# Two fused feed-forward blocks behind a retention layer: another order of block products, activations split on VectorE, first form weights loaded earlier

## The chip, the core and the metric

The kernel runs on one core of one Trainium2 chip. The metric is the time of one execution on the device in microseconds (us). Engines are named as in the profile: PE is TensorE (PEld its weight loads), DVE is VectorE, ACT is ScalarE, POOL is GpSimd, SP is SyncE, which here only issues DMAs.

## What is computed

```python
# retention: state = gamma * state + k v^T ; y = scale * q state   (4 batches, 8 heads, 768 steps, 64 wide)
x = attn_out.transpose(0, 2, 1, 3).reshape(B * S, H * D)        # 3072 x 512
h = x @ moe_w_in            # 512 -> 2048
g = np.maximum(0.01 * h, h)
x = g @ moe_w_out           # 2048 -> 512
h = x @ moe2_w_in           # 512 -> 2048
g = h - np.tanh(h)
return g @ moe2_w_out       # 2048 -> 512
```

Everything is float32. A product of float32 matrices is made of three matmuls on split operands: high part by high part, high by low and low by high, where the high part is the value rounded to the matmul's format and the low part is the rest.

## The kernel before

After the retention layer come four matrix products. The two that widen (512 to 2048) are done by a Strassen-Winograd scheme: a group is a pair of 128-row blocks of the hidden dimension, and instead of eight block products it takes seven, P1 to P7 (table PROD: form of the weight, form of the activation, PSUM bank). One block product is 6 matmuls of 128x128 by 128x512. The two that narrow (2048 to 512) are outer products: step o takes one 128-row block of activations and adds to four PSUM banks, in two halves of 6 matmuls each. The first narrowing product is o = 0 to 95, the second o = 96 to 191.

The stretch that the change is about starts when 48 outer products of the first narrowing product are done (ND_FROM). From there on PE alternates: 168 block products of the second widening product (24 groups d of seven, built by `prod`) and 288 halves of outer products (`half_unit`), about 1.7 halves behind each product, until the products are used up; 56 halves and one more are left for the end. A product or a half is called a unit here: 456 units, the last 57 without products.

What stands around a unit:

- Weights. The seven forms of a group were made earlier by DVE and ACT (`form_sets`) and stored to DRAM (`wfs`, `put_forms`, 7 DMAs on SP). `load_f(i)` loads the weights `wf` of product i, four products ahead (F_AHEAD).
- Activations of outer product o. `load_g` loads `gr`, three outer products ahead; `split_g(o + 2)` makes the high part `gh` on ACT (L151) and the low part `gl` = gr - gh on an engine that it is told (L152): DVE up to o = 49, POOL after that.
- Results of a group. The bank X of group d (two banks in turn) holds P1, then on top of it P6, P7 and P4; Y (one bank) holds P5, then P3; Z holds P2. ACT copies the sum after P1, P5 and P6 to SBUF (`kp`, L889), and DVE adds: P2 with the copy of P1, P3 with that of P6, P7 with that of P5 (`h`, L896). P4 ends in the bank and is read there. A product that adds to a bank waits for the copy or addition that still reads it.
- Elementwise. From each of the four sums of a group h - tanh(h) is made (`queue_el`): four ACT instructions (`eu`, `et`, `es`, `mk`), on DVE `ew` twice (L924, L927), `es` (L930) and a predicated copy (L942), for three of four a DMA on POOL that adds h to `et` (L958). The result is stored (`g2s`) and comes back as `gr` of the second narrowing product.
- Weights of the second narrowing product: `second_out` makes `w2h` (ACT, L823) and `w2l` (DVE, L825) from `w2r`.

Everything is written in program order by a planner. After each unit `background` adds a credit of 1.29 us x 1.05 to each of "a" (ACT) and "v" (DVE), capped at 2.0; copies and additions of due products are written at once and charged; then the other queues are written as long as their credit is over zero, in this order for DVE: forms of the next activations (`bx`), elementwise, then weight forms, `second_out` and conversions. ACT's and DVE's work runs in the order so written, each engine in turn. SBUF tiles come from a list of free slots, first in, first out (`alloc`, `give`); a tile waits for the last reader of its slot.

The order of the seven products of a group is written in line 798; P4' stands for P4 of the group before.

Of the kernel before, what the change touches and what calls it, by code (L numbers as in the profile page):

```python
# [9 lines left out]
F32 = mybir.dt.float32  # L10
F32R = mybir.dt.float32r
# [44 lines left out]
PROD = {  # L56
    "P1": ("A11", "B11", "X", 0),
    "P2": ("A12", "B21", "Z", 1),
    "P5": ("S1", "T1", "Y", 2),
    "P6": ("S2", "T2", "X", 4),  # L60
    "P3": ("S4", "B22", "Y", 5),
    "P7": ("S3", "T3", "X", 10),
    "P4": ("N22", "T4", "X", 13),
}
FORMS = ("A11", "A12", "S1", "S2", "S3", "S4", "N22")
NG = NM // 2
NSB = NC // 2
SPAN = 7 * NG

ND_FROM, N_TAIL, UNIT_US = 3 * NM, 28, 1.29  # L70
C_AHEAD, M_AHEAD, F_AHEAD, F_LOW = 5, 3, 4, 5
# [3 lines left out]
def kernel(  # L75
# [12 lines left out]
    nc = tc.nc  # L88
# [17 lines left out]
    wfs = dr.tile([NG, 7, P, 2, 2 * P], F32, tag="wfs", name="wfs")  # L106
# [5 lines left out]
    def alloc(nm, dt=F32, shape=(P, TB)):  # L112
        pool, tag = free.popleft()
        serial[0] += 1
        t = pool.tile(list(shape), dt, tag=tag, name=f"{nm}_{serial[0]}")
        home[id(t)] = (t, pool, tag)
        return t

    def give(*ts):
        for t in ts:  # L120
            _, pool, tag = home.pop(id(t))
            free.append((pool, tag))
# [5 lines left out]
    def run(queues, us):  # L128

        while us > 0:  # L130
            for queue in queues:
                cost = next(queue[0], "end") if queue else None
                if cost is not None:
                    break
            if cost is None:
                return 0.0
            if cost == "end":
                queue.popleft()
            else:
                us -= cost  # L140
        return us
# [7 lines left out]
    def split(hi, lo, src, eng):  # L149

        nc.scalar.activation(out=hi, in_=src, func=AF.Copy)  # L151
        eng.tensor_tensor(out=lo, in0=src, in1=hi.bitcast(F32), op=ALU.subtract)  # L152
# [57 lines left out]
    def conversion(units, ready=None, ahead=RAW_BUFS - 1):  # L210

        while ready and not ready():
            yield None
        last = len(units)
        at = {}
        raws[0] += 1

        def load(n):
            if n < last:
                units[n].load()  # L220
                at[n] = tick[0] + LOAD_LEAD

        for n in range(ahead):
            load(n)
        for n in range(last + 2):
            if n >= 2:
                yield from units[n - 2].done(units[n - 2])
            if n < last:
                while tick[0] < at[n] or len(free) < 3:
                    yield None  # L230
                units[n].s1()
            if 1 <= n <= last:
                yield from units[n - 1].s2()
                load(n - 1 + ahead)
        raws[0] -= 1
# [33 lines left out]
    formed = set()  # L269
# [356 lines left out]
    def where_g(o):  # L626

        if o < NT:
            return o // NM, o % NM
        nb, i = divmod(o - NT, NM)  # L630
        return nb, i // 2 + i % 2 * NG

    def load_g(o):
        if o < 2 * NT:
            nb, m = where_g(o)
            assert o < NT or (nb, m) in made2, (nb, m)
            GR[o] = alloc("gr")
            nc.sync.dma_start(out=GR[o], in_=(g1s if o < NT else g2s)[nb, m])

    def split_g(o, eng):  # L640
        if o < 2 * NT:
            G[o] = alloc("gh", F32R), alloc("gl", F32R)
            split(*G[o], GR[o], eng)
            give(GR.pop(o))

    def mm_half(o, half):
        nb, m = where_g(o)
        first, last = o % NM == 0, o % NM == NM - 1
        js = (2 * half, 2 * half + 1)
        base = 0 if o // NM in (1, 2 * NC - 1) else 4  # L650
        g = G[o]
        for j in js:
            if first:
                ACC[j] = bank(base + j, f"o_{o // NM}_{j}")
            c = slice(j * P, (j + 1) * P)
            if o < NT:
                w = WO[m]
                three = ((w[0][:, c], g[0]), (w[0][:, c], g[1]), (w[1][:, c], g[0]))
            else:
                w = WE[m]  # L660
                three = ((g[0][:, c], w[0]), (g[0][:, c], w[1]), (g[1][:, c], w[0]))
            for i, (a, b) in enumerate(three):
                nc.tensor.matmul(ACC[j], a, il(b), start=first and i == 0, stop=last and i == 2)  # L663
        if half:
            give(*G.pop(o))
            if nb == NC - 1 and o < NT:
                give(*WO.pop(m))
# [20 lines left out]
    def step(o):  # L688
        for half in range(2):
            mm_half(o, half)  # L690
            evac(o, half)
# [74 lines left out]
    for i, (at_, sb, g, nm) in enumerate(stream):  # L766
# [13 lines left out]
        if xleft:  # L780
            c, p = xleft.pop(0)
            t = xw.pop((c, p))
# [12 lines left out]


    dnow = [-1]
    order = [(d, nm) for d in range(NSB * NG) for nm in ("P1", "P4'", "P2", "P5", "P6", "P3", "P7")]
    order = [(d - 1, "P4") if nm == "P4'" else (d, nm) for d, nm in order if nm != "P4'" or d]
    order.append((NSB * NG - 1, "P4"))  # L800
    place = {x: i for i, x in enumerate(order)}
    NPROD = len(order)
# [3 lines left out]
    def second_out():  # L806
        rl, arrive = {}, {}

        def fetch(i):
            if i < NM:  # L810
                rl[i] = alloc("w2r")
                nc.sync.dma_start(out=rl[i], in_=w2s[use_in[i]])
                arrive[i] = tick[0] + LOAD_LEAD

        fetch(0)
        fetch(1)
        for i, m in enumerate(use_in):
            fetch(i + 2)
            while tick[0] < arrive[i] or len(free) < 10:
                yield None  # L820
            hi, lo = alloc("w2h", F32R), alloc("w2l", F32R)
            src = rl[i].rearrange("p (b a) -> p a b", a=2)
            nc.scalar.activation(out=hi.rearrange("p (a b) -> p a b", a=2), in_=src, func=AF.Copy)  # L823
            yield 0.0
            nc.vector.tensor_tensor(out=lo.rearrange("p (a b) -> p a b", a=2), in0=src,  # L825
                                    in1=hi.rearrange("p (a b) -> p a b", a=2).bitcast(F32), op=ALU.subtract)
            give(rl.pop(i))
            WE[m] = hi, lo
            yield 0.7

    conv.append(conversion(conv2_in + conv2[W2_EARLY:]))
    at_n = [0]
# [21 lines left out]
    for n in range(ND_FROM):  # L854
        load_g(n + C_AHEAD if n + C_AHEAD < ND_FROM + M_AHEAD else 2 * NT)
        if n == 0:
            split_g(2, nc.vector)
            continue
        while n % NM not in WO:
            tick[0] += 1  # L860
            run((conv,), 0.01)
        step(n)
        at_n[0] = n
        split_g(n + 2, nc.vector)
        tick[0] += 2
        us = run((loads, bx, forms, conv), min(us + 1.85, 1.9))


    FW, KP, XB = {}, {}, {}

    def load_f(i):
        if i < NPROD:
            d, nm = order[i]
            assert d % NG in formed, d
            t = alloc("wf", F32R)
            nc.sync.dma_start(out=t.bitcast(F32).rearrange("p (n c) -> p n c", n=2), in_=wfs[d % NG, FORMS.index(PROD[nm][0])])  # L876
            FW[i] = t

    events = {}

# [112 lines left out]
    credit = {"a": 0.0, "v": 0.0}  # L993
# [26 lines left out]
    def background():  # L1020
        for f in events.pop(tick[0], ()):
            a, v = f()
            credit["a"] -= a
            credit["v"] -= v
        credit["a"] = min(credit["a"] + UNIT_US * 1.05, 2.0)
        credit["v"] = min(credit["v"] + UNIT_US * 1.05, 2.0)
        run((loads,), 0.01)
        spend((bx,))
        while (masks[0] < 2 and drain(mk_q, "a")) or drain(act_q, "a"):
            pass  # L1030
        while drain(cp_q, "v") or drain(dve_q, "v"):
            pass
        spend((forms, bo, conv) if tick_o[0] >= NT - 14 else (forms, conv))

    tick_o = [ND_FROM]
    for i in range(F_AHEAD):
        load_f(i)
    split_done = [ND_FROM + 2]
    halves = deque((o, half) for o in range(ND_FROM, 2 * NT) for half in range(2))
    n_mid = len(halves) - 2 * N_TAIL  # L1040
    i = gone = since = 0

    def half_unit():
        o, half = halves.popleft()
        tick_o[0] = o
        if half == 0:
            load_g(o + M_AHEAD)
        while o >= NT and where_g(o)[1] not in WE:
            tick[0] += 1
            background()  # L1050
        mm_half(o, half)
        tick[0] += 1
        evac(o, half)
        if half == 0:
            split_g(o + 2, nc.gpsimd)
        background()

    while i < NPROD or halves:
        if i < NPROD:
            d, nm = order[i]  # L1060
# [9 lines left out]
        while halves and (i == NPROD or gone < i * n_mid / NPROD):  # L1070
            o, half = halves[0]
# [59 lines left out]
```

## Time and profile before

| what | us |
|---|---|
| median of 3 runs | 1110.67 |
| lowest and highest run | 1108.86, 1111.59 |
| the profiled execution, its own time | 1111.41 |
| its span, first to last instruction | 1109.6 |
| PE busy | 1061.0 (96%) |
| DVE busy | 826.4 (74%) |
| ACT busy | 691.5 (62%) |
| POOL busy | 294.1 (27%) |

The profiled execution lasts 1.8 us longer than its span. The shares are means over a retention stretch (to about 120 us), the first widening and narrowing products, the mixed stretch from 475 us to 1032 us and an end of outer products alone; they say little of any of these.

### The profile page before, as it was taken

The numbers are of one execution on the slowest core, as the hardware profiler recorded it, in microseconds if no ns is written. First come the engines' busy times: TensorE is split into PE (matmuls) and PEld (weight loads), VectorE is DVE, ScalarE is ACT, GpSimd is POOL, SyncE is SP. The second block draws the span as 40 slices with busy tenths as digits, with TensorE's granted clock in tenths as the row PEclk, the third lists the DMA queues.
The fourth block names the chain that finished last, engine by engine and source line by source line (L and its number), as shares of the span: only waits on it lengthen the run. The fifth ranks groups of instructions, "written<-read, shape, count | busy, mean of one in ns | idle before, by whom it ended". The sixth has DMA issues, their size and how long they took to land. (4 is left out here: it accounts for less than half of the span.)

```text
span 1109.6 us, 17689 instructions
## 1 busy us (share of the span) xinstructions
PE 1061.0 (96%) x5931; PEld 911.5 (82%) x5931; DVE 826.4 (74%) x1221; ACT 691.5 (62%) x1227; POOL 294.1 (27%) x266
## 2 busy tenths in 40 slices
PE   9999899999999999889799998889999899999998
PEld 6888778888888888777688886778888788888887
DVE  3578897766888797969888789888779977677400
ACT  5766667756775555546666666776667666667540
POOL 3222000000000000023434343334334443445651
PEclk9999999999999999989899999999999999999999
DMA  9997464674769699498999986888987878888540
GB/s 223 241 268 189 165 234 176 222 266 162 257 231 306 223 377 357 167 302 280 295 299 266 300 255 190 275 253 250 280 285 194 258 228 254 228 246 262 184 162 38
DMA packets 208635, 267.68 MB, mean 241 GB/s; under 512 B 65056, under 2 KB 106144, under 8 KB 208544
## 3 DMA queue, kind: packets, MB, share of 16 engines
q1 hardware_dynamic: 197888, 247.52, 66.8%
q0 software_dynamic: 10368, 18.88, 9.8%
q8 instruction: 47, 0.77, 0.3%
q14 instruction: 44, 0.36, 0.1%
q10 hardware_dynamic: 288, 0.15, 0.1%
HBM read 161.63 MB, written 85.98 MB: 223 GB/s over the span
## 5 line engine op out<-in xcount | busy, mean ns | idle before, releaser
L152 POOL TENSOR_TENSOR gl<-gr,gh 128x512 fp32r<-128x512 f32 x142 | 201.5, 1426 | 650.2 <-ACT gh L151 619.8
L663 PE MATMUL o<-gh,wo 128*128 128x512 f32 x768 | 241.2, 381 | 2.9 <-ACT gh L151 2.9
L151 ACT ACTIVATE gh<-gr 128x512 fp32r<-128x512 f32 x192 | 118.6, 624 | 103.8 <-DMA gr<-g1s 47.0
L663 PEld LDWEIGHTS o<-gh,wo 128*128 128x128 f32 x768 | 146.1, 190 | 24.3 <-ACT gh L151 3.6
L978 PE MATMUL Xd<-xch,wf 128*128 128x512 f32 x384 | 131.8, 384 | 19.5 <-DVE h L896 8.5
L663 PE MATMUL o<-gl,wo 128*128 128x512 f32 x384 | 146.9, 382 | 1.6 <-POOL gl L152 1.2
L663 PE MATMUL o<-w2h,gl 128*128 128x512 f32 x384 | 145.7, 380 | 1.6 <-POOL gl L152 1.6
L663 PE MATMUL o<-w2h,gh 128*128 128x512 f32 x384 | 145.8, 380 | 1.4 <-ACT st L676 1.4
L663 PE MATMUL o<-w2l,gh 128*128 128x512 f32 x384 | 145.5, 379 | 0.0
L722 PE MATMUL X<-xch,wg 128*128 128x512 f32 x384 | 123.3, 381 | 3.8 <-DVE wg L166 2.6
L942 DVE COPY_PREDICATED es<-mk,et 128x512 f32<-128x512 uint16 x96 | 91.6, 962 | 41.1 <-ACT mk L920 36.8
L978 PEld LDWEIGHTS Xd<-xch,wf 128*128 128x128 f32 x384 | 73.1, 190 | 33.8 <-DVE h L896 10.9
L927 DVE SCALAR_TENSOR_TENSOR ew<-eu,ew 128x512 f32<-128x512 f32 x96 | 89.6, 933 | 3.1
L722 PEld LDWEIGHTS X<-xch,wg 128*128 128x128 f32 x384 | 72.4, 189 | 17.2 <-DVE wg L166 3.4
L908 ACT ACTIVATE eu<-h 128x512 f32<-128x512 f32 x72 | 45.0, 625 | 66.2 <-DVE h L896 65.8
L930 DVE SCALAR_TENSOR_TENSOR es<-es,ew 128x512 f32<-128x512 f32 x96 | 81.1, 844 | 5.3 <-ACT gh L151 0.5
L663 PEld LDWEIGHTS o<-gl,wo 128*128 128x128 f32 x384 | 73.0, 190 | 14.0 <-POOL gl L152 2.1
L958 POOL DMA_DIRECT2D et<-h x72 | 63.2, 886 | 77.1 <-ACT et L912 36.3
L663 PEld LDWEIGHTS o<-w2h,gl 128*128 128x128 f32 x384 | 72.6, 189 | 12.8 <-POOL gl L152 2.4
L663 PEld LDWEIGHTS o<-w2h,gh 128*128 128x128 f32 x384 | 72.6, 189 | 12.4 <-ACT st L676 1.8
L663 PEld LDWEIGHTS o<-w2l,gh 128*128 128x128 f32 x384 | 72.6, 189 | 10.2
L978 PE MATMUL Yd<-xch,wf 128*128 128x512 f32 x192 | 66.9, 389 | 9.2 <-ACT kp L889 9.0
(103 smaller groups left out, 2101.8 us busy)
## 6 DMA issues: line engine op xcount, KB each, us to landing
wf<-wfs SPq DMA_DIRECT2D x168, 256.0 KB, 4.6
g1s<-c SPq DMA_DIRECT2D x96, 256.0 KB, 2.2
gr<-g1s SPq DMA_DIRECT2D x96, 256.0 KB, 5.2
g2s<-es SPq DMA_DIRECT2D x96, 256.0 KB, 2.9
gr<-g2s SPq DMA_DIRECT2D x96, 256.0 KB, 4.5
et<-h POOLq DMA_DIRECT2D x72, 256.0 KB, 4.9
raw<-in_moe_w_in_dram SPq DMA_DIRECT2D x32, 512.0 KB, 5.7
raw<-in_moe_w_out_dram SPq DMA_DIRECT2D x32, 512.0 KB, 4.5
```

Of the source, the lines that this page charges most:

```text
L151: nc.scalar.activation(out=hi, in_=src, func=AF.Copy)
L152: eng.tensor_tensor(out=lo, in0=src, in1=hi.bitcast(F32), op=ALU.subtract)
L663: nc.tensor.matmul(ACC[j], a, il(b), start=first and i == 0, stop=last and i == 2)
L722: nc.tensor.matmul(ps, w[:, c], il(x), start=first and kt == 0 and i == 0, stop=kt == 1 and i == 2, skip_group_check=True)
L908: nc.scalar.activation(out=e["u"], in_=h, func=AF.Square)
L927: nc.vector.scalar_tensor_tensor(out=e["w"], in0=e["u"], scalar=A1, in1=e["w"], op0=ALU.add, op1=ALU.mult)
L930: nc.vector.scalar_tensor_tensor(out=e["s"], in0=e["s"], scalar=K1, in1=e["w"], op0=ALU.add, op1=ALU.mult)
L942: nc.vector.copy_predicated(out=e["s"], mask=e["mk"].bitcast(mybir.dt.uint16), data=e["th"])
L958: nc.gpsimd.dma_start(out=e["th"], in_=h, accum_op=ALU.add)
L978: nc.tensor.matmul(ps, a, il(b), start=nm in ("P1", "P2", "P5") and kt == 0 and j == 0, stop=kt == 1 and j == 2, skip_group_check=True)
```

## The change

Three edits. The order of the products of a group is P1, P5, P4', P6, P2, P3, P7 in place of P1, P4', P2, P5, P6, P3, P7. The low parts `gl` of outer products 50 to 191 are made by DVE, and the planner charges both engines for a split. The first four weight loads stand behind the last four steps of the loop before the mixed stretch, in place of behind that loop.

```diff
-    order = [(d, nm) for d in range(NSB * NG) for nm in ("P1", "P4'", "P2", "P5", "P6", "P3", "P7")]
+    order = [(d, nm) for d in range(NSB * NG) for nm in ("P1", "P5", "P4'", "P6", "P2", "P3", "P7")]
...
         step(n)
         at_n[0] = n
         split_g(n + 2, nc.vector)
+        if ND_FROM - F_AHEAD <= n:
+            load_f(n - ND_FROM + F_AHEAD)
         tick[0] += 2
...
     tick_o = [ND_FROM]
-    for i in range(F_AHEAD):
-        load_f(i)
     split_done = [ND_FROM + 2]
...
         evac(o, half)
         if half == 0:
-            split_g(o + 2, nc.gpsimd)
+            split_g(o + 2, nc.vector)
+            credit["a"] -= 0.63
+            credit["v"] -= 0.69
         background()
```

`load_f` itself is the same and only stands further up. Three places show what moves.

SP's queue where the mixed stretch begins, before the change: the weights `wf` of the first products stand behind the stores of a group's forms (`wfs`).

```order
L288 DMA wfs<-wg_5087 128x2x256
L288 DMA wfs<-wg_5088 128x2x256
L290 DMA wfs<-wg_5089 128x512
L876 DMA wf_5331<-wfs 128x512
L876 DMA wf_5333<-wfs 128x512
L876 DMA wf_5335<-wfs 128x512
L876 DMA wf_5337<-wfs 128x512
L876 DMA wf_5346<-wfs 128x512
```

The same queue now: three of the four loads stand ahead of the stores `x2s` of the last outer product's results, the fourth behind these and ahead of the forms.

```order
L638 DMA gr_5223<-g1s 128x512
L838 DMA wf_5241<-wfs 128x512
L638 DMA gr_5252<-g1s 128x512
L838 DMA wf_5270<-wfs 128x512
L838 DMA wf_5292<-wfs 128x512
L678 DMA x2s<-st_5303 128x512
L678 DMA x2s<-st_5306 128x512
L678 DMA x2s<-st_5315 128x512
L678 DMA x2s<-st_5318 128x512
L838 DMA wf_5325<-wfs 128x512
L288 DMA wfs<-wg_5083 128x2x256
```

They have moved past those stores and the seven stores of forms; the load of `gr` for outer product 50 now has one of them ahead.

DVE's work in the second group, before: elementwise instructions alone.

```order
L927 SCALAR_TENSOR_TENSOR ew_5910<-eu_5856,ew_5910 128x512
L930 SCALAR_TENSOR_TENSOR es_5869<-es_5869,ew_5910 128x512
L924 SCALAR_TENSOR_TENSOR ew_5937<-eu_5888,Xd_5582 128x512
L927 SCALAR_TENSOR_TENSOR ew_5937<-eu_5888,ew_5937 128x512
L934 TENSOR_TENSOR et_5890<-Xd_5582,et_5890 128x512
L930 SCALAR_TENSOR_TENSOR es_5892<-es_5892,ew_5937 128x512
```

And now: a `gl` about every six instructions, each of which reads the `gh` that ACT makes from the loaded `gr`.

```order
L152 TENSOR_TENSOR gl_5879<-gr_5829,gh_5878 128x512
L944 COPY_PREDICATED es_5748<-mk_1_5866,et_5739 128x512
L926 SCALAR_TENSOR_TENSOR ew_5900<-eu_5822,h_5789 128x512
L929 SCALAR_TENSOR_TENSOR ew_5900<-eu_5822,ew_5900 128x512
L944 COPY_PREDICATED es_5797<-mk_1_5892,et_5795 128x512
L932 SCALAR_TENSOR_TENSOR es_5842<-es_5842,ew_5900 128x512
L152 TENSOR_TENSOR gl_5920<-gr_5870,gh_5919 128x512
L926 SCALAR_TENSOR_TENSOR ew_5924<-eu_5894,Xd_5573 128x512
```

On DVE whatever stands behind a `gl` now waits with it for ACT and for the load of `gr`.

DVE's work where the second narrowing product begins, as it stands now: `w2l_7810` belongs to the weights of outer product 97, `gl_7820` behind it to the activations of outer product 99.

```order
L944 COPY_PREDICATED es_7687<-mk_1_7800,et_7685 128x512
L825 TENSOR_TENSOR w2l_7810<-w2r_7073,w2h_7809 128x512
L152 TENSOR_TENSOR gl_7820<-gr_7776,gh_7819 128x512
L825 TENSOR_TENSOR w2l_7829<-w2r_7075,w2h_7828 128x512
L944 COPY_PREDICATED es_7728<-mk_9_7824,et_7726 128x512
```

The weights of outer product 97 are thus written right ahead of their use, those of 98 and 99 three units and one unit ahead; before, it was 23, 22 and 24 units.

## Rows read from the trace of the kernel before

**Rows 1.** Chain that ended last, its last piece: start us, us, what.

```profile
1031.73 73.83 PE o L663 x342
```

**Rows 2.** PE's instructions in time, 455 to 490 us: start, length, what [idle before, releaser].

```profile
466.73 0.38 PE L663 MATMUL o<-gh,wo 128*128 128x512 f32 x1
475.45 0.76 PE L978 MATMUL Xd<-xch,wf 128*128 128x512 f32 x1 [8.35 <-DMA wf<-wfs]
...
480.18 0.38 PE L663 MATMUL o<-gh,wo 128*128 128x512 f32 x1
```

**Rows 3.** SP's DMA issues in time, 430 to 490 us.

```profile
465.89 2.20 SPq L678 DMA_DIRECT2D x2s<-st  x4
...
472.05 2.69 SPq L876 DMA_DIRECT2D wf<-wfs  x5
```

**Rows 4.** PE's waits from 480 to 1040 us: us in total, times, longest.

```profile
PE Yd L978 <- ACT kp L889: 9.0, 6, 2.2
PE Xd L978 <- DVE h L896: 8.5, 6, 2.7
PE o L663 <- ACT gh L151: 2.9, 1, 2.9
PE o L663 <- POOL gl L152: 2.8, 4, 0.9
PE o L663 <- ACT st L676: 1.4, 1, 1.4
PE Xd L978 <- ACT kp L889: 1.4, 2, 1.0
PE Xd L978 <- DVE et L934: 1.3, 1, 1.3
```

**Rows 5.** PE's instructions in time, 530 to 552 us.

```profile
534.79 0.38 PE L978 MATMUL Xd<-xch,wf 128*128 128x512 f32 x1
...
548.24 0.38 PE L663 MATMUL o<-gl,wo 128*128 128x512 f32 x1
```

**Rows 6.** Groups of DVE, 480 to 1040 us: shapes, xcount, busy us, mean ns, idle before.

```profile
L942 DVE COPY_PREDICATED es<-mk,et 128x512 f32<-128x512 uint16 x95 | 90.8, 964 | 41.0 <-ACT mk L920 36.6 <-DMA et<-h 4.2
L927 DVE SCALAR_TENSOR_TENSOR ew<-eu,ew 128x512 f32<-128x512 f32 x96 | 89.6, 933 | 3.1
L930 DVE SCALAR_TENSOR_TENSOR es<-es,ew 128x512 f32<-128x512 f32 x96 | 81.1, 844 | 5.3 <-ACT gh L151 0.5
L924 DVE SCALAR_TENSOR_TENSOR ew<-eu,h 128x512 f32<-128x512 f32 x72 | 64.8, 901 | 4.3 <-DMA wfs<-wg 2.8 <-ACT eu L908 1.6
...
L896 DVE TENSOR_TENSOR h<-Zd,kp 128x512 f32<-128x512 f32 x24 | 16.4, 683 | 12.4 <-PE Zd L978 9.3 <-DMA out_dram<-st 2.5 <-DMA g2s<-es 0.6
```

**Rows 7.** DVE and POOL in time, 655 to 690 us.

```profile
669.38 0.73 DVE L942 COPY_PREDICATED es<-mk,et 128x512 f32<-128x512 uint16 x1
...
669.94 1.89 POOL L152 TENSOR_TENSOR gl<-gr,gh 128x512 fp32r<-128x512 f32 x1 [0.53 <-ACT gh L151]
...
670.72 1.66 DVE L927 SCALAR_TENSOR_TENSOR ew<-eu,ew 128x512 f32<-128x512 f32 x1
...
672.41 0.69 DVE L930 SCALAR_TENSOR_TENSOR es<-es,ew 128x512 f32<-128x512 f32 x1
```

**Rows 8.** Groups of POOL, 480 to 1040 us.

```profile
L152 POOL TENSOR_TENSOR gl<-gr,gh 128x512 fp32r<-128x512 f32 x119 | 172.9, 1454 | 631.1 <-ACT gh L151 607.3 <-DMA g2s<-es 6.1 <-DMA wf<-wfs 5.4
```

**Rows 9.** Groups of DVE, 120 to 440 us.

```profile
L152 DVE TENSOR_TENSOR gl<-gr,gh 128x512 fp32r<-128x512 f32 x39 | 26.3, 684 | 15.1 <-ACT gh L151 15.1
```

**Rows 10.** Busy us (instructions) in two stretches: PE, PEld, DVE, ACT, POOL, PEclk, DMA, GB/s.

```profile
467.00:605.00 138.00, 121.78 (x532) 103.63 (x532) 115.05 (x159) 85.18 (x150) 52.24 (x41) 0.93 0.92 292
655.00:745.00 90.00, 76.99 (x343) 63.66 (x342) 77.35 (x103) 62.75 (x110) 30.75 (x27) 1.00 0.77 237
```

**Rows 11.** ACT's waits from 480 to 1040 us.

```profile
ACT gh L151 <- DMA gr<-g2s: 35.7, 20, 5.8
ACT gh L151 <- DMA gr<-g1s: 33.0, 15, 5.0
```

More of the change, by code (lines that the diff above doesn't have):

```diff
@@ L829, in second_out, with load_f @@
             yield 0.7
+    FW, KP, XB = {}, {}, {}
+    def load_f(i):
+        if i < NPROD:
+            d, nm = order[i]
+            assert d % NG in formed, d
+            t = alloc("wf", F32R)
+            nc.sync.dma_start(out=t.bitcast(F32).rearrange("p (n c) -> p n c", n=2), in_=wfs[d % NG, FORMS.index(PROD[nm][0])])
+            FW[i] = t
     conv.append(conversion(conv2_in + conv2[W2_EARLY:]))
@@ L864 @@
         split_g(n + 2, nc.vector)
+        if ND_FROM - F_AHEAD <= n:
+            load_f(n - ND_FROM + F_AHEAD)
         tick[0] += 2
         us = run((loads, bx, forms, conv), min(us + 1.85, 1.9))
[L869 to L877, printed above, removed]
     events = {}
```

## The prediction, made before the changed kernel ran

> **What bounds the kernel now.** I read PE first, since it is busy 96% of the span. The chain's last piece gives its pace: 342 matmuls without a pause in 73.83 us [rows 1], so 0.2159 us a matmul and 1.295 us a unit. From the last outer product before the mixed stretch (its last matmul starts at 466.73 [rows 2]) to 1031.73 [rows 1] stand 456 - 57 = 399 units: 516.7 us at that pace, and 564.8 us (less one matmul's 0.2) passed. So PE loses **48.1 us** there, and that is all that this change can win; what lies before and after it keeps its place.
>
> Three places make up the 48.1.
> - The first product waits 8.35 us for its weights, and then runs slow: its row lasts 0.76 us where 0.38 is usual, and 12 matmuls that need 2.59 us end at 480.18 [rows 2]. From 466.95 to 480.18 that is 13.23 - 2.59 = **10.6 us**. The reader should see on SP's queue why: five weight loads are issued at 472.05, behind the stores of x2 and of seven forms [rows 3].
> - From 534.79 to 548.24, 13.45 us, only 17 matmuls start [rows 5], worth 3.67: **9.8 us**, a wait for `gh` with slow matmuls behind it (granted clock 0.93 in the whole of 467 to 605 [rows 10], so partly at the lower of 1.2 and 2.4 GHz).
> - The rest, **27.7 us**, is some 18 short waits: products that wait for ACT's copies or DVE's additions (9.0, 8.5, 1.4 and 1.3 us in all), outer products that wait for `gl` and `gh` [rows 4]. About 0.3 us each comes on top of the gap that the row shows, as the engine refills.
>
> Behind the short waits stands DVE. Its groups in the mixed stretch have means of 964, 933, 844 and 901 ns, but the additions from PSUM 683 [rows 6]. In time one sees why: the copy takes 0.73 us alone, L930 0.69 us alone, and L927 lasts 1.66 us while POOL works on a `gl` from 669.94 on [rows 7]. The planner reckons 0.7 us, so DVE falls behind what it planned.
>
> **The change, part by part.**
>
> *First weights.* The four DMAs now stand ahead of the forms' stores, three of them also ahead of x2's, whose issue begins at 465.89 [rows 3]. The first two are then issued before PE ends outer product 47, and the wait and the slow matmuls behind it go: -10.6 us. Late next would be the weights of the fifth product: still behind the seven stores, so issued about 472, used at 467 + 10 units = 480. That leaves 8 us, and the row of PE shows no later weight wait [rows 4]. The `gr` loads moved behind a weight load lose one issue, 0.5 us (five take 2.69 [rows 3]), against a use 9 us later: nothing.
>
> *`gl` from POOL to DVE.* DVE gains 119 instructions in this stretch [rows 8] at 684 ns, as the same line took on DVE earlier [rows 9]: +81.4 us. It loses the lengthening: against 0.73 and 0.69 us [rows 7] that is 95 x 0.23 + 96 x 0.24 + 96 x 0.15 + 72 x 0.21 [rows 6] = 74 us, and some 8 us in smaller groups that I estimate at the same tenth-part of their time. Net about **0 us** of DVE time, and the planner now books the true amount. 23 more `gl` fall at the end, where DVE has nothing to do and PE loses nothing: nothing either way.
> The page "SBUF — State Buffer" of the Trainium skill, section "SBUF: two separate sides", says that DVE instructions with two SBUF inputs and a GpSimd instruction that reads SBUF take turns under an exclusive lock, the loser blocked entirely. The trace agrees, 1.66 against 0.69 us, and the additions with one input in PSUM stay at 683 ns. If every one of the 119 held DVE for its whole 1.454 us, the change would take 173 us off DVE and it would come out 92 us lighter; the rows say 0.
>
> *What this leaves.* PE's stall-free need and DVE's work nearly meet. From 467 to 605 PE loses 10.6 + 9.8 + about 3, so 88.5 units pass: 114.6 us of PE against 115 us of DVE. From 655 to 745 about 14.5 us are lost, 58.3 units or 75.5 us of PE against 77.4 us of DVE [rows 10]. So in these stretches DVE stays a few us behind, and waits of its own come on top. Losses shrink; they don't vanish.
>
> *The order.* In units between the instruction that frees a bank and the product that needs it, as the built order has them: P3 behind the copy of P5 from 3 or 4 to 8 or 9; P6 and P7 behind copies, smallest from 2 to 4; P4 behind the addition of P7, typically from 3 or 4 to 6. These are the waits of 9.0, 1.4 and 8.5 us [rows 4]. What pays: P5 behind the addition of P3 falls from 11 to 6 units (7.8 us), and P1 of the group after next behind the elementwise reads of P4 from 10 to 8, but to **0** at two places (units 148 and 281, where the forms of the next activations are built).
>
> Remaining losses, term by term:
> - copies: 10.4 us of gap, 12.5 with refills; with 8 units = 10 us of air I keep 1.5.
> - additions: 8.5, 10 with refills; I keep half, 5, for P5's new place and the full stretches.
> - P1 behind P4's reads: now 1.3, 1.6 with refill. Two places at zero units: each costs DVE's lag, 3 us (DVE exceeds PE by about 2 us in such a stretch) and one 0.69: 7 for both. Bounds 1.6 and, at the longest single ACT wait of 5.8 each [rows 11], 12.
> - `gl` and `gh`: 5.7 of gap, with refills and the slow matmuls (some 3) about 10 now. DVE's queue delivers `gl` later than an idle POOL, slots are scarcer near the start (the list of free ones runs down to 0, from 3), but the lag is smaller: I keep 6. Bounds 0 and 13 (7 more, as for the lag at P1).
> - ACT's emptying of banks: 1.7, stays.
> - `w2l` right ahead of use at outer products 97 to 99: new. Two instructions in a row, 1.4 us at 684 ns each, plus lag of 2 to 3 us: 4.5. Bounds 0 and 9.
>
> Sum 25.7 against 48.1: **-22.4 us**. The profiled execution took 1111.4 us (span 1109.6), 0.7 above the median of 1110.67; 1111.4 - 22.4 = **1089 us**.
>
> **The rivals.**
> - *A, nearly all goes.* DVE follows its plan, lag stays under 6 units everywhere, the slow spot doesn't recur; only 8 us of loss remain (ACT's emptying, the two zeros). 1111.4 - 40 = 1071. For it: contention was the only thing that the planner didn't know. Against: DVE's 100 to 102% in two stretches.
> - *B, half is handed back.* The first weights pay, the rest returns as waits for `w2l`, zero-unit banks and late slots: 40 us stay, 1103. For it: the upper bounds above; they add up to some 42.
> - *C, slower.* DVE waits in order behind `gl` for `gh` and so for the load of `gr`. On POOL that wait of 607 us was free [rows 8]. ACT waits 68.7 us for `gr` over 119 splits [rows 11]; in the two full stretches, 147 of 399 units, that is 25 us which DVE cannot make up, and PE would lose 25.7 + 25 = 51 us; with one more slow spot of 9.8 [rows 5] it loses 61. 1111.4 + 13 = 1124. It decides from 22 us of such waits on. Against: earlier, DVE's wait for `gh` came to 15.1 us for 39 `gl` [rows 9], 0.39 each, 17 us for the 43 in full stretches, and a DVE that is behind finds `gh` done.
> - *D, no change.* The stalls only move: PE gains 10.6 at the start and loses it at `w2l` and the zero-unit banks, each at its upper bound, with the old losses kept: 48 back, 1111.
>
> **How the numbers follow.** Forecast (1080 to 1098 around 1089) 0.53, A 0.18, B 0.16, D 0.06, C 0.07. A measurement of this kernel can tell 0.3%, 3.3 us, from no change. Faster takes the forecast, A and B: 0.87; same D: 0.06; slower C: 0.07. The range keeps forecast and B, and half of A: **1072 to 1106**; outside lie half of A, C and D.
>
> **What would show it.** At 467 us no weight wait and no slow matmuls: first step right. DVE groups L924 to L944 at 0.67 to 0.74 us with POOL left with its DMAs: second right; if they stay near 0.9, another cause stretches them. Waits of Yd for `kp` under 2 us in all: order right. Waits near outer products 97 to 99 for `w2h` or `w2l`, and of Xd at the change of activations, of 2 to 5 us each: the terms that I added. The forecast is wrong if DVE's wait for `gh` exceeds 22 us where it is full (C), or if PE's short waits still sum to over 35 us.

## The result, and the profile after

The changed kernel takes **1121.89 us** (median of 4 runs, 1120.03 to 1123.95) against 1110.61 us for the kernel before on the same chip (1108.86 to 1111.59): a ratio of 1.0104, with a 95% interval of 1.008 to 1.0127. It is 1.0% slower. The forecast was 1089 us, in a range of 1072 to 1106, with a chance of 0.07 for slower.

Line numbers of the mixed stretch are 2 higher after the change (L934 is L936, L978 is L980); the loads of form weights moved from L876 to L838.

First the end of the chain of waits of the changed kernel (start us, us, what). The last piece has the same length as before, and begins 12.6 us later [rows 1]. So what was lost was lost ahead of that piece.

```profile
1044.34 73.83 PE o L663 x342
```

Next SP's issues in time. The first form weights are now issued from 451.99 on, three of them ahead of the x2 stores and the fourth behind these, where all came at 472.05 before [rows 3].

```profile
451.99 0.32 SPq L838 DMA_DIRECT2D wf<-wfs  x1
...
458.61 2.91 SPq L838 DMA_DIRECT2D wf<-wfs  x2
465.29 2.26 SPq L678 DMA_DIRECT2D x2s<-st  x4
467.64 0.42 SPq L838 DMA_DIRECT2D wf<-wfs  x1
```

PE starts its first product at 466.40 without a wait. But at 483.25 it waits for `gh`, because ScalarE has waited 7.97 us for a load of `gr`: two `gr` loads are issued only at 475.16, behind the seven stores of forms.

```profile
466.19 0.38 PE L663 MATMUL o<-gh,wo 128*128 128x512 f32 x1
466.40 0.38 PE L980 MATMUL Xd<-xch,wf 128*128 128x512 f32 x1
...
483.25 0.48 PE L663 MATMUL o<-gh,wo 128*128 128x512 f32 x1 [2.43 <-ACT gh L151]
```

```profile
482.56 0.63 ACT L151 ACTIVATE gh<-gr 128x512 fp32r<-128x512 f32 x1 [7.97 <-DMA gr<-g1s]
```

VectorE's groups between 480 and 1040 us (shapes, count, busy us, mean ns, idle before). The means fell from 964, 933, 844 and 901 ns [rows 6] to 738, 690, 687 and 683. The lower parts stand in the first row, and ahead of them VectorE waits 90.8 us for ScalarE's `gh`.

```profile
L152 DVE TENSOR_TENSOR gl<-gr,gh 128x512 fp32r<-128x512 f32 x114 | 78.4, 688 | 96.3 <-ACT gh L151 90.8 <-DMA g2s<-es 5.3
L944 DVE COPY_PREDICATED es<-mk,et 128x512 f32<-128x512 uint16 x92 | 67.6, 738 | 6.6 <-ACT mk L922 4.1 <-DMA et<-h 2.4
L929 DVE SCALAR_TENSOR_TENSOR ew<-eu,ew 128x512 f32<-128x512 f32 x92 | 63.5, 690 | 2.7
L932 DVE SCALAR_TENSOR_TENSOR es<-es,ew 128x512 f32<-128x512 f32 x92 | 63.2, 687 | 2.7
L926 DVE SCALAR_TENSOR_TENSOR ew<-eu,h 128x512 f32<-128x512 f32 x70 | 47.8, 683 | 0.0
```

PE's waits between 480 and 1040 us, whole list (total, times, longest). The waits for copies `kp`, 10.4 us before, and nearly all for additions `h`, 8.5 us before [rows 4], are gone. In their place stands the first row: three waits of Xd for `et`.

```profile
PE Xd L980 <- DVE et L936: 25.3, 3, 9.3
PE o L663 <- ACT gh L151: 6.3, 5, 2.4
PE o L663 <- DVE gl L152: 3.1, 7, 1.1
PE Xd L980 <- DMA wf<-wfs: 2.4, 2, 1.5
PE o L663 <- DVE w2l L825: 2.2, 1, 2.2
PE Xd L980 <- ACT et L914: 1.8, 1, 1.8
PE o L663 <- ACT st L683: 1.2, 1, 1.2
PE o L663 <- ACT w2h L823: 0.6, 1, 0.6
PE Yd L980 <- DVE h L898: 0.5, 1, 0.5
```

L936 is the second of the two VectorE instructions that read P4 out of PSUM (`v1` at L926, `v4` at L936). P1 of the group two later needs the same X bank and waits for them at 522, 692 and 889 us, 6.7, 9.3 and 9.3 us. The middle one in time, first on PE and then on VectorE (start, length, what, [idle before, releaser]):

```profile
682.53 0.38 PE L663 MATMUL o<-gh,wo 128*128 128x512 f32 x1
692.18 0.79 PE L980 MATMUL Xd<-xch,wf 128*128 128x512 f32 x1 [9.27 <-DVE et L936]
...
697.84 0.38 PE L980 MATMUL Yd<-xcl,wf 128*128 128x512 f32 x1
```

```profile
673.56 1.29 DVE L369 TENSOR_TENSOR xq_B<-xq_B,xq_B 128x512 f32<-128x512 f32 x2
674.94 1.30 DVE L166 TENSOR_TENSOR xcl<-xq_B,xch 128x512 fp32r<-128x512 f32 x2
...
682.87 0.68 DVE L152 TENSOR_TENSOR gl<-gr,gh 128x512 fp32r<-128x512 f32 x1
...
687.10 0.69 DVE L152 TENSOR_TENSOR gl<-gr,gh 128x512 fp32r<-128x512 f32 x1 [1.03 <-ACT gh L151]
...
689.50 0.68 DVE L926 SCALAR_TENSOR_TENSOR ew<-eu,Xd 128x512 f32<-128x512 f32 x1
690.22 0.69 DVE L929 SCALAR_TENSOR_TENSOR ew<-eu,ew 128x512 f32<-128x512 f32 x1
690.83 0.72 DVE L944 COPY_PREDICATED es<-mk,et 128x512 f32<-128x512 uint16 x1
691.45 0.68 DVE L936 TENSOR_TENSOR et<-Xd,et 128x512 f32<-128x512 f32 x1
```

VectorE had built the next activations until 676 (L369, L166). While PE stands still it works through older elementwise instructions, two lower parts and a wait of 1.03 us, and reads P4 last. From 692.18 to 697.84, 5.66 us, PE starts 13 matmuls, worth 2.81 us at the usual pace, so 2.85 us more are lost behind the pause. The next windows (us of the window, PE, PEld, DVE, ACT, POOL busy, granted clock, DMA, GB/s) show why: with no matmul running the clock falls to its lower level, 0.50 or 1.2 GHz, and it is full again only in the last of these windows.

```profile
684.00:690.00 6.00, 0.00 (x0) 0.00 (x0) 4.96 (x9) 4.60 (x9) 1.51 (x2) 0.80 1.06 279
690.00:696.00 6.00, 3.82 (x9) 3.10 (x10) 2.09 (x4) 1.64 (x4) 0.86 (x1) 0.50 0.99 266
696.00:702.00 6.00, 6.00 (x25) 5.08 (x25) 4.23 (x7) 2.59 (x5) 0.00 (x0) 0.85 0.04 14
702.00:708.00 6.00, 6.00 (x30) 5.25 (x29) 4.73 (x9) 4.04 (x8) 0.00 (x0) 1.00 0.67 219
```

The sum: from the start of the last matmul before the mixed stretch (466.19) to 1044.34 pass 578.15 us, less one matmul's 0.22, against a need of 516.7, so PE loses 61.2 us where it lost 48.1. Its pauses in the list above come to 43.4 us, 25.3 of them the three, and one of 0.5 us stands before 480. The other 17.3 are the remainder, matmuls at the lower clock and refills, not measured one by one.

### The profile page after: what moved, and what is told of

Its sections match the earlier page's. It is cut to its first block, busy times and chain, and to the rows that moved or that the text cites. A ratio compares the mean times of both kernels' runs of the same rounds, so it can differ in the third digit from the quotient of the medians.

```text
span 1122.2 us, 17512 instructions
## 1 busy us (share of the span) xinstructions
PE 1065.5 (95%) x5931; PEld 915.6 (82%) x5931; DVE 830.8 (74%) x1363; ACT 694.2 (62%) x1227; POOL 93.2 (8%) x124
## 5 line engine op out<-in xcount | busy, mean ns | idle before, releaser
L152 DVE TENSOR_TENSOR gl<-gr,gh 128x512 fp32r<-128x512 f32 x192 | 130.7, 687 | 138.2 <-ACT gh L151 132.7
L980 PE MATMUL Xd<-xch,wf 128*128 128x512 f32 x384 | 134.5, 392 | 30.0 <-DVE et L936 25.3
L980 PEld LDWEIGHTS Xd<-xch,wf 128*128 128x128 f32 x384 | 74.8, 195 | 44.2 <-DVE et L936 26.5
L944 DVE COPY_PREDICATED es<-mk,et 128x512 f32<-128x512 uint16 x96 | 70.4, 738 | 6.6 <-ACT mk L922 4.1
L980 PE MATMUL Xd<-xcl,wf 128*128 128x512 f32 x192 | 74.8, 390 | 0.0
L722 PE MATMUL X<-xcl,wg 128*128 128x512 f32 x192 | 72.8, 379 | 0.0
L922 ACT ACTIVATE mk<-eu,lead 128x512 bf16<-128x512 f32 x96 | 68.4, 716 | 1.3 <-DVE es L944 1.3
```

Source lines behind the costliest of these rows:

```text
L722: nc.tensor.matmul(ps, w[:, c], il(x), start=first and kt == 0 and i == 0, stop=kt == 1 and i == 2, skip_group_check=True)
L922: nc.scalar.activation(out=e["mk"], in_=e["u"], func=AF.Relu, bias=edge)
L944: nc.vector.copy_predicated(out=e["s"], mask=e["mk"].bitcast(mybir.dt.uint16), data=e["th"])
L980: nc.tensor.matmul(ps, a, il(b), start=nm in ("P1", "P2", "P5") and kt == 0 and j == 0, stop=kt == 1 and j == 2, skip_group_check=True)
```

## The experiments

Theory A: the loss is these three waits, since P4's reads come too late in VectorE's program. Theory B, rival C of the prediction: VectorE waits in order for `gh`, with its other work behind it. Theory C: the new order is bad by itself. Theory D came up later: the charge of 0.63 and 0.69 us makes VectorE's work late everywhere, so a wait that is removed turns up elsewhere. Each run was compared with the kernel before on its own chip (medians 1111.35 to 1112.79 us). Differences between runs below are differences of medians, partly from different chips; by the ratios some come out 1 to 2 us larger.

### The three parts of the change, apart

**e1_early_weights**: the loads alone.

```diff
+        if ND_FROM - F_AHEAD <= n:
+            load_f(n - ND_FROM + F_AHEAD)
...
-    for i in range(F_AHEAD):
-        load_f(i)
```

> Theory A (late reads): the changed kernel loses its time at three places where P1 of a group waits for the X bank until VectorE has read P4 of the group two before from it; these waits (25.3 us, and some 10 us more at a lowered clock around them) need the new order together with the lower parts on VectorE. Theory B (waits in order): the lower parts on VectorE cost the time by themselves, because VectorE waits there 132.7 us for ScalarE's gh with its other work behind it. Theory C (order): the new order costs it by itself. This run has the first four form weights loaded sooner and nothing else: the wait of 8.35 us at 475 and the 2.2 us before it go, so all three expect 1111 - 10 = 1100 us (1097 to 1104).

1105.29 us, ratio 0.9951 (0.9934 to 0.9969): 5 to 6 us, half of what was expected, and slower than the range. The wait of 8.35 us is gone, but its list of waits (480 to 1040 us) now begins with

```profile
PE Yd L980 <- ACT kp L891: 15.1, 9, 3.4
```

against 9.0 us before [rows 4]. A likely reason, not shown, is that PE comes sooner to the copies, which ScalarE doesn't finish sooner.

**e2_order_only**: the order alone.

```diff
-("P1", "P4'", "P2", "P5", "P6", "P3", "P7")
+("P1", "P5", "P4'", "P6", "P2", "P3", "P7")
```

> The new order alone, lower parts still on GpSimd, first weights late. Theories A and B: the short waits for copies and additions (Yd and Xd behind kp and h, 19 us before) shrink by some 12 us; P1 has 2 and 3 products' time at the two close places, and VectorE owes some 3 us there, so a few us go back: 1111 - 12 + 4 = 1103 us (1098 to 1109). Theory C: the three long waits of 7 to 9 us are there: 1111 - 12 + 35 = 1134 us (1120 to 1140).

1106.13 us, ratio 0.9945 (0.9926 to 0.9964), inside the range of A and B; theory C falls. The waits for copies shrink to 1.1 us, and two short waits for P4's reads stand at the two close places, at 686 and 871 us:

```profile
PE Xd L978 <- DVE et L934: 6.7, 2, 3.4
```

**e5_early_and_order**: everything but the lower parts, which stay on GpSimd and uncharged.

```diff
-            split_g(o + 2, nc.vector)
-            credit["a"] -= 0.63
-            credit["v"] -= 0.69
+            split_g(o + 2, nc.gpsimd)
```

> The changed kernel with the lower parts back on GpSimd and without their charge to the two budgets; new order and early weights stay. Theories A and B: no wait of P1 behind P4 over 3 us, 1103 - 10 = 1093 us (1088 to 1099), so that the lower parts on VectorE cost 29 us. Theory C: the long waits stay, 1122 us (1117 to 1127).

1102.01 us, ratio 0.9921 (0.9893 to 0.9948). This misses the 1088 to 1099 of A and B, and the two waits behind P4 come to 7.2 us, the longer to 3.9; it is far from C's 1117. So loads and order together give 9 us, and the third part of the change takes that and 11 us more.

**e6_no_charge**: the lower parts on VectorE, without the two lines of the charge.

```diff
             split_g(o + 2, nc.vector)
-            credit["a"] -= 0.63
-            credit["v"] -= 0.69
```

> The changed kernel without the charge of 0.63 and 0.69 us to the two budgets: the lower parts stay on VectorE, but P4's reads are put into VectorE's program sooner (7, 3 and 2 products ahead of P1 at the close places, in place of 3, 0 and 0), with more work queued ahead of them (by the durations of its instructions up to 17 us where it was 8). Theory A, place in the program alone: the three long waits go, 1090 us (1084 to 1097). Theory A, place plus the queue ahead: waits of a few us at more places, 1115 us (1105 to 1125). Theory B: as the changed kernel, 1122 us (1118 to 1128), VectorE still waiting over 100 us for gh.

1102.73 us, ratio 0.9921 (0.9904 to 0.9938). It lies between A's two ranges, in neither, and far from B's. Two numbers in two lines of the planner are thus worth 19 us. Moving the lower parts from GpSimd to VectorE is worth nothing by itself (1102.01 and 1102.73). VectorE still waits 81.4 us for `gh` in 480 to 1050 us, hardly less than the 90.8 of the changed kernel, while PE's waits behind P4's reads fall from 25.3 to 7.6 us:

```profile
L152 DVE TENSOR_TENSOR gl<-gr,gh 128x512 fp32r<-128x512 f32 x126 | 86.6, 688 | 84.0 <-ACT gh L151 81.4 <-DMA wf<-wfs 2.2
```

```profile
PE Xd L980 <- DVE et L936: 7.6, 2, 4.7
```

### Size of the charge, and what goes first

**e8_half_charge**: 0.32 and 0.34 in place of 0.63 and 0.69.

> The changed kernel with half the charge (0.32 and 0.34 us). P4's reads stand 2 and 1 products ahead of P1 at the close places (none with the whole charge, 3 and 2 with none), while VectorE owes about 6 us there (3 and 7.5). Theory A: two waits of 4 to 6 us in place of 9.3 and of 3.0 and 4.7: 1106 us (1103 to 1112), nearer to the kernel without the charge (1103) than to the one with all of it (1122). Rival D, in which the time goes with the charge: 1112 us (1109 to 1116).

1100.62 us, ratio 0.9895 (0.9874 to 0.9916), better than A expected, and by their intervals not to be told from no charge. The two waits are as expected, longer than without a charge and shorter than with the whole one (first row below); what all other waits come to is 13.2 us, against 14.9 without a charge.

```profile
PE Xd L980 <- DVE et L936: 11.4, 2, 5.8
PE o L663 <- ACT gh L151: 5.3, 4, 1.7
```

**e7_bx_behind**: whole charge, all elementwise work ahead of the next activations.

```diff
-        spend((bx,))
         while (masks[0] < 2 and drain(mk_q, "a")) or drain(act_q, "a"):
             pass
         while drain(cp_q, "v") or drain(dve_q, "v"):
             pass
+        spend((bx,))
```

> The changed kernel with the charge kept, and the budget spent on the elementwise queues ahead of the building of the next activations (ahead of it before). P4's reads are then 7 to 8 products' time ahead of P1 at the two places where there was none (units 148 and 281), and the place at unit 31 stays. Theory A (the long waits of P1 behind P4's reads are the loss, since the charged budget goes to the next activations first): the waits at 692 and 889 (18.6 us) and some 6 us of lowered clock go: 1122 - 24 = 1098 us (1094 to 1107). Rival D (the charge makes VectorE's work late everywhere, so what is put ahead only makes something else late): the activations' lower parts become the wait, 1115 to 1122 us.

1117.07 us, ratio 1.0034 (1.0022 to 1.0046): in D's range and not in A's. The waits at 692 and 889 are gone, as A said, but the activations became the wait, 9.0 + 5.4 + 4.4 + 2.4 = 21.2 us, of which three rows:

```profile
PE Yd L980 <- ACT xch L160: 9.0, 2, 5.1
PE Xd L980 <- DVE et L936: 6.4, 1, 6.4
PE Xd L980 <- DVE xcl L166: 5.4, 4, 3.0
```

**e11_p4_reads_first**: whole charge, and only the two reads of P4 ahead.

```diff
+            if in_psum:
+                ps_q.extend([(t, 0.7, v1), (t, 0.7, v4)])
+                dve_q.append((t, 0.7, v2))
+            else:
+                dve_q.extend([(t, 0.7, v1), (t, 0.7, v2)])
...
+        while drain(ps_q, "v"):
+            pass
         spend((bx,))
```

> The changed kernel with the whole charge and its own order; only the two VectorE instructions that read P4 out of PSUM get a queue of their own, spent ahead of the next activations and of all other elementwise work. By the built order they then stand 6 or more products ahead of P1 at the places that had none, 4 at the first place. Theory A (these two reads are the loss): the waits of 6.7, 9.3 and 9.3 us shrink to under 2 each, and some 8 us of half clock behind them go: 1122 - 22 - 8 = 1092 us (1088 to 1099). Rival D (the charge keeps work out of VectorE's program, so the wait turns up elsewhere, as it did on the activations when all elementwise work was put ahead of them): 1115 us or more.

1106.59 us, ratio 0.9951 (0.9936 to 0.9967). The edit takes 48 VectorE instructions ahead, with what the budget then shifts behind them, and 15 of the 19 us come back (17 of 20 by the ratios). So the late place of these two reads causes most of the loss, as A has it. A's number was still missed by 8 us, and D's by as much: 25.3 us of waits became 3.4, yet the time fell by 15 and not by 30. All pauses together went from 43.4 to 27.5 us, so other waits grew by 6: ScalarE's emptying of banks (`st`) from 1.2 to 3.9 us in two rows, `w2h` from 0.6 to 2.2, the additions `h` from 0.5 to 1.9, `gh` from 6.3 to 7.3. Of its list:

```profile
PE o L663 <- ACT gh L151: 7.3, 7, 1.9
PE Xd L982 <- DVE et L936: 3.4, 1, 3.4
...
PE o L663 <- ACT st L676: 2.9, 2, 1.6
...
PE o L663 <- ACT w2h L823: 2.2, 1, 2.2
```

**e12_reads_first_half**: the same edit with half the charge.

> The same with half the charge. The run with half the charge took 1100.6 us, and lost 11.4 us in two waits behind P4's reads and some 5 us of half clock behind them. Theory A: 1100.6 - 16 = 1085 us (1082 to 1091). Rival D: the waits move, 1098 us or more.

**1097.29 us**, ratio 0.9865 (0.9844 to 0.9887): the fastest kernel of the study, 15 us under the kernel before and some 25 under the changed one. It lies between A's range and D's, 0.7 us below D's and 6 above A's: the 11.4 us of waits behind P4's reads went, all other waits grew from 13.2 to 21.1 us, and 3 us were gained (the intervals with and without the edit, 0.9844 to 0.9887 and 0.9874 to 0.9916, still overlap). No pause of PE after 480 us is longer than 2.1 us, and the clock stays full where it had fallen, at 0.55, in the run with half the charge:

```profile
684.00:690.00 6.00, 5.70 (x27) 4.68 (x26) 5.62 (x10) 4.18 (x8) 0.86 (x1) 1.00 0.85 227
690.00:696.00 6.00, 6.00 (x30) 5.15 (x29) 5.93 (x10) 5.57 (x10) 0.00 (x0) 1.00 0.89 276
```

**e13_reads_first_none** and **e14_reads_first_gpsimd**: the same edit without a charge, with the lower parts on VectorE and on GpSimd.

> The same with no charge. The run without the charge took 1102.7 us, and lost 7.6 us in two waits behind P4's reads and some 5 us of half clock. Theory A: 1090 us (1086 to 1096). Rival D: 1100 us or more.

> Early weights, new order, lower parts on GpSimd with no charge, and P4's reads first. The run without this took 1102.0 us, with 7.2 us in two waits behind P4's reads and some 3 us of half clock behind them. Theory A: 1092 us (1088 to 1097). If the lower parts on VectorE are worth nothing by themselves, this run and the one before with no charge differ by less than 3 us; if VectorE's longer instructions beside GpSimd still cost, it is 4 us or more slower.

1102.60 us (ratio 0.9914, 0.9893 to 0.9935) and 1103.11 us (0.9911, 0.9887 to 0.9936). No wait for P4's reads is left in either, and neither gained: D was right here. Where 7.6 us of P4's waits went, other waits grew by about as much in the first, `gh` from 4.7 to 8.7 us and Yd for `h` from 0.2 to 3.5:

```profile
PE o L663 <- ACT gh L151: 8.7, 6, 3.2
...
PE Yd L982 <- DVE h L898: 3.5, 2, 3.3
```

The two runs are 0.5 us apart, although GpSimd stretches VectorE's copies from 738 to 949 ns, here first with the lower parts on VectorE, then on GpSimd:

```profile
L944 DVE COPY_PREDICATED es<-mk,et 128x512 f32<-128x512 uint16 x96 | 70.3, 738 | 4.2 <-ACT mk L922 3.1 <-ACT eu L910 1.0 <-DMA et<-h 0.2
```

```profile
L944 DVE COPY_PREDICATED es<-mk,et 128x512 f32<-128x512 uint16 x96 | 90.1, 949 | 20.8 <-ACT mk L922 16.0 <-ACT es L918 1.9 <-DMA et<-h 1.3
```

The Trainium skill's page "SBUF — State Buffer", section "SBUF: two separate sides", has a GpSimd instruction that reads SBUF and a VectorE instruction with two SBUF inputs shut each other out; the rows agree that VectorE is held up, by 0.21 us a copy. The equal times don't show that this costs nothing. The four groups of elementwise work take 318 us in the second run and 252 in the first, but the first has 82 us of lower parts on VectorE where the second has 8, so one load was exchanged for another of about the same size.

### Another order

**e9_p4_first** and **e10_p4_first_no_charge**.

```diff
-("P1", "P5", "P4'", "P6", "P2", "P3", "P7")
+("P4'", "P1", "P5", "P6", "P2", "P3", "P7")
```

> The changed kernel, charge and all, in the order P4 of the group before, P1, P5, P6, P2, P3, P7: P4 comes two products sooner than in the changed kernel, the rest of its order stays. Its reads then stand 2 products ahead of P1 at the close places, where VectorE owes 4 us, and 6 at the first place; some lower parts of the second layer's weights stand right ahead of their use. Theory A: two waits of 3 to 5 us in place of three of 6.7 to 9.3, and a few us for those weights: 1106 us (1099 to 1111). Rival D: no gain from the place alone, 1118 us or more.

> As the run before, and without the charge: P4's reads stand 7 products ahead of P1 at the close places with some 8 us owed, so no wait behind them is longer than 1 us; the additions on the Y bank have the least room (8 to 9 products, 11 to 18 us of queued work). Theory A: the kernel without the charge (1103) less its two waits behind P4 (7.6 us) and some 2 us of clock: 1094 us (1089 to 1102). If instead the queue on VectorE (up to 18 us) decides, the waits move to the Y bank and the time stays at 1103 us.

1118.40 us (ratio 1.0055, 1.0031 to 1.0079) and 1132.72 us (1.0178, 1.0153 to 1.0203). Neither tells A from D, because the order brought a wait that both expectations overlooked: P4 adds onto the X bank that holds P7, so it must follow VectorE's addition that reads P7, and here it comes directly behind P7. These waits come to more without the charge, where by the expectation more work is queued ahead of that addition (not checked in the trace). First with the charge, then without:

```profile
PE Xd L980 <- DVE h L898: 26.5, 10, 6.9
```

```profile
PE Xd L980 <- DVE h L898: 42.6, 15, 7.4
```

## Why the prediction was wrong, point by point

- **First weights: mechanism right, size half.** The wait went, and later weight waits come to 2.4 us in all, the longest 1.5. Alone it gave 5 to 6 us, not 10.6, while the waits of Yd for copies grew by 6.1. The question that was put to the fifth weight was not put to the `gr` loads, which were counted as nothing: behind the same seven stores they made ScalarE wait 7.97 us and PE 2.43.
- **Lower parts on VectorE: "Net about 0 us" was right, and what stands behind it was the first wrong step.** The shorter durations came as forecast, and the move is worth 0.7 us one way or the other (e5 and e6). But "the planner now books the true amount" was counted as harmless. The charge takes its amount out of a budget that is spent on the next activations first; what is late then is P4's reads. With the two lines of the charge gone the time fell by 19 us (e6).
- **P1 behind P4's reads, "7 for both", was the term that failed.** The zero distance at units 148 and 281 was found in the built order, and P1 waited there. The price was wrong: VectorE's mean lag of 3 us and one instruction of 0.69, with an upper bound of 12 for both; measured were 9.3 each. What counts there is the queue ahead of those two instructions right after the next activations are built, on which VectorE works from 676.16 to 691.45. A third place, at unit 31 (3 units, 6.7 us), was not priced. And each pause took PE to the lower clock for some microseconds more, which this term left out, though the kernel before shows it (0.93 in 467 to 605, [rows 10]).
- **The rest of the sum came out near by luck.** Without that term the forecast had 25.7 - 7 = 18.7 us of losses left; the list shows 43.4 - 25.3 = 18.1: copies none (1.5 forecast), additions 0.5 (5), `gl` and `gh` 9.4 (6), ScalarE's emptying 1.2 (1.7), `w2h` and `w2l` 2.8 (4.5), others 4.2, which had no term. The misses cancel, and the forecast's terms hold refills and slow matmuls, which the list does not.
- **A reading of the kernel before.** The slow spot from 534.79 to 548.24 was read as a wait for `gh`; of its pauses that one has 2.87 us, a wait for a copy 2.23 and one for `gl` 0.55.
- **Rival C, the slower one, had the sign and not the cause.** In the two full stretches (467 to 605 and 655 to 745) VectorE waited 22.7 + 12.7 = 35.4 us for `gh`, over the 22 us from which this was to decide, and C's 61 us of loss and 1124 us are close to what was measured. That is luck: the run without the charge waits 24.0 + 6.3 = 30.3 us there, also over 22, and is 19 us faster. These waits by themselves don't decide.
- **No run reached 1089 us.** The terms were added as if each wait could be removed by itself. In these runs half or less came: 5 to 6 of 10.6 (e1), 3 of 16 (e12) and 15 of 30 (e11), both with the expected gain in clock, nothing of 7.6 (e13).

Left open: which of the two charges does it (VectorE's alone was not run, nor the charge with the lower parts on GpSimd), and why half the charge is better than none when P4's reads come first (0.9865 against 0.9914, intervals just apart). The profiled executions, 9.3 us apart, show in part where the time goes: the waits come to 21.1 us with half the charge and to 25.1 with none, and the mean granted clock was 1.000 against 0.993, by estimate at most 7.7 us (0.007 of a span of 1104.8).

## What to carry to other kernels

Where a planner spends a budget in a fixed order of priority, a new charge is not bookkeeping: it moves what stands last in that order, so look for the instruction there that frees a bank or a buffer for PE, and put it first. Price such a wait by the work queued ahead of the freeing instruction at that very place, not by the engine's mean lag, and add the lower clock behind a long pause. When several waits stand close behind one another, expect half or less of what a removed wait shows. Tune the charge too: half of the true amount in place of all of it was worth 21 us here, and 9 with P4's reads first, while putting these first was worth 15 us with the whole charge, 3 with half and none without.

## What the runs showed of the hardware that was not expected

A pause of 9.27 us cost more than itself: the granted clock was 0.50 in the 6 us around PE's restart at 692.18, 0.85 in the next 6 and 1.00 only then, while in the fastest run pauses of up to 2.1 us left it at 1.00. The length of one pause does not decide alone: in e13 a pause of 2.03 us, ending at 483.75, was followed by a granted clock of 0.51 from 486 to 489 us, and in the kernel before one of 2.69, ending at 692.75, by 1.00. And VectorE's elementwise instructions were a fifth to a third longer beside GpSimd, copies 949 against 738 ns, 66 us in the four groups of e14 against e13; taking this away by giving VectorE GpSimd's work left the kernel's time the same.
